# Loads of gate/up weights moved from the end of a block's gate/up into the projections and W2's passes, with new places for key copies, Wo rows, residual tiles and packs

## The chip, the cores and the metric

The kernel runs on one NeuronCore of a Trainium2 chip. TensorE (PE) multiplies, VectorE (DVE), ScalarE (ACT) and GpSimd (POOL) do the elementwise work, and SyncE (SP) issues nearly all DMAs, in the order in which they stand in its program. The metric is the device time of one execution in microseconds; shorter is better.

## What is computed

A layer norm, sliding-window attention and a gated MLP, added to the input:

```python
def _A_ref(x, wqkv, wo):                   # H = 32 heads of Dh = 18, window W = 256
    q, k, v = ...                          # x @ wqkv, split into heads
    scores = einsum("bhqd,bhkd->bhqk", q, k) * Dh**-0.5
    mask = (i - j >= 0) & (i - j < W)
    p = softmax(where(mask, scores, -1e9))
    return (p @ v) @ wo
def _B_ref(x, w1, w3, w2):
    return (silu(x @ w1) * (x @ w3)) @ w2  # 576 -> 4608 -> 576
xn = layernorm(x)                          # x: 1 x 2048 x 576, bf16
return x + _A_ref(xn, A_wqkv, A_wo) + _B_ref(xn, B_w1, B_w3, B_w2)
```

## The kernel before

The 2048 rows are worked in four blocks of 512 (the loop over `c`, line 1296). Each block goes through three stages on TensorE.

**Gate/up.** 36 units (`u`), each 128 of the 4608 hidden columns: nine pairs of matmuls of W3 and W1 with the transposed, normalized input (`unit_pairs`, L855), then ScalarE's tanh (L864) and two VectorE operations that form the gated value (L870, L873). Between the pairs stand the scores, exponentials and masks of attention and, at fixed units, the products of probabilities with V ("PV", L734). In block 0 two PV products stand together in unit 27; the second writes PSUM banks that unit 26 used and VectorE's L873 must free. Four units use one set of W3/W1 columns. A set comes from HBM in four parts (two DMAs of 320 KB and two of 256 KB; the first two sets in six smaller ones) into one of three buffers (`load_part`, L339). Nine sets make a block; block 0's nine come first, and the first two of the next block are asked for at the end of the block ahead.

**Projections.** Q, K and V of the next block (`proj_begin`, L492), nine passes in the order of `PROJ` with a list index `m`. VectorE and ScalarE cast the results to `stage`; from there small DMAs repack queries (`new_q`, from ScalarE's queue) and keys (`new_k`, L633: eight copies of 72, 18 and 9 KB) to the layout that scores need.

**W2's passes.** Four 32-row lanes of TensorE run side by side, in rounds (`w2_lanes`). An output slice of 128 columns takes 36 matmuls of W2 a lane (L1031) and then four or five with Wo's rows and the packed attention output `oT` (L1040). Scores of the next block's first heads are mixed in. W2 comes in pieces of 288 KB into four buffers (`load_w2`, L375); a piece serves nine rounds, and its buffer is asked for again when all four lanes are through with it. Four pieces are loaded ahead in gate/up, so a slice's four pieces are there at the start and the fifth piece, the first of the second slice, is the first that the stage itself loads. The last 64 columns follow in L1081, and a last PV product ends the stage.

What sets the order of DMAs is the order of calls: `add("sp", ...)` appends an instruction to SyncE's program, with waits for the last writer or reader of each buffer. SyncE waits at an instruction until its semaphores are there, and nothing behind it is issued meanwhile. Four places decide it here:

- In gate/up, `owed += 4` at every fourth unit asks for a set; `owe_part` then issues one of its parts after the fourth and the ninth pair of a unit, each waiting for TensorE to come that far.
- `later(u, ...)` puts packs (`o_pack`, L812: four copies of the attention output of two head groups to `oT`), residual additions and stores at fixed units.
- `if c == 0 and u == ...` places block 0's one-time work: the clear of the new-key buffer `kn`, the eight copies of block 0's last 256 keys into it (`first_prev`, L648), Wo's rows (L1465, L1476, L1479) and `wz` (L1481). The normalized tiles of block 1 are transposed by DMA (`xn_send`, L449); a tile buffer `xn0` or `xn1` is written again (L424) only after its transpose has landed.
- In W2's passes a dictionary by round number, `events`, places repacks of the older heads' queries and keys (`span_main`, L580, and `span_last`, L611) and loads of residual tiles (L307).

```python
                if u % 4 == 3 and u < NF - 4 and (c or u != 15) or c and u == 0:
                    owed += 4
```

## Time and profile before

| what | value |
|---|---|
| median of three runs | 557.95 us (556.53 to 558.99) |
| the profiled execution: its time / its span | 558.62 us / 556.9 us |
| TensorE busy | 548.9 us (99%) |
| VectorE / ScalarE / GpSimd busy | 66% / 53% / 22% |
| the chain of work that ended last | PE 94%, DMA 3%, SyncE's queue 1% |
| granted TensorE clock | full throughout |
| gate/up, blocks 0, 1, 2 | 81.7, 75.9, 75.9 us |
| projections, for blocks 1, 2 | 13.8, 13.2 us |
| W2's passes, blocks 0, 1, 2 | 47.6, 45.5, 45.5 us |
| DMA traffic | 88.13 MB, mean 158 GB/s |

All times in the views are microseconds from the start of the span. "SPq" is an issue by SyncE's queue: its start, how long the issue took, and the transfer; the transfer lands later, and "us to landing" counts from the issue's start. A row of a timeline with "x4" holds four neighbours that were merged. "DMA share" is the mean busy share of sixteen DMA engines in a window. Idle time of TensorE is put in brackets with the one that ended it.

### The profile page before, as it was taken

How to read it: one execution, taken by the hardware profiler on the slowest of the kernel's cores; microseconds unless marked ns; L12 is line 12 of the kernel's file. 1: busy time of each engine (PE TensorE's matmuls, PEld its weight loads, DVE VectorE, ACT ScalarE, POOL GpSimd, SP SyncE). 2: the span in 40 equal slices, each digit the busy share in tenths (PEclk: the TensorE clock that was granted, in tenths of full speed). 3: DMA queues.
4: the chain of work that ended last, by engine and by line, in shares of the span. 5: the costliest groups of instructions: out<-in, count | busy, mean ns of one | idle time of the engine just before them, and what ended most of it. 6: DMA issues, size and time to landing. Idle time of an engine off the chain costs nothing.

```text
span 556.9 us, 17711 instructions
## 1 busy us (share of the span) xinstructions
PE 548.9 (99%) x7690; PEld 305.6 (55%) x7690; DVE 365.4 (66%) x745; ACT 294.2 (53%) x481; POOL 120.1 (22%) x281
## 2 busy tenths in 40 slices
PE   8999998989999999999999999999999999999998
PEld 4555554568564444455556444445555644545776
DVE  6566988735747889674664888866465686676211
ACT  6557765348735554536782555443787355554000
POOL 5524645100003332120001242320000222211000
PEclk9999999999999999999999999999999999999999
DMA  9997968967747996994793799697577488662552
GB/s 244 184 207 147 209 146 161 208 148 159 163 68 172 205 206 116 207 181 112 147 168 82 172 209 195 133 208 145 141 148 118 109 191 173 165 150 79 137 151 64
DMA packets 167031, 88.13 MB, mean 158 GB/s; under 512 B 102506, under 2 KB 164714, under 8 KB 166954
## 3 DMA queue, kind: packets, MB, share of 16 engines
q1 hardware_dynamic: 165834, 85.42, 74.6%
q10 hardware_dynamic: 1120, 1.59, 1.0%
q8 instruction: 60, 0.98, 0.8%
q14 instruction: 17, 0.14, 0.1%
HBM read 71.30 MB, written 2.36 MB: 132 GB/s over the span
## 4 chain that ended last, share of the span: by engine, by line
PE 94%; DMA 3%; SPq 1%; DVE 0%; issue 0%
PE ps L855 50%; PE ps L1031 17%; PE ps L492 8%; PE ps L927 6%; PE ps L677 4%; PE ps L1081 2%; PE ps L734 2%; PE ps L1040 2%; PE ps L786 2%; DMA pt<-in_A_wqkv_dram 1%; PE ps L751 1%; DMA w<-in_B_w_dram 1%; PE ps L934 1%; DMA kn<-stage 1%; SPq L633 0%
## 5 line engine op out<-in xcount | busy, mean ns | idle before, releaser
L855 PE MATMUL ps<-xnT,w 64*128 64x512 bf16 x1400 | 177.8, 376 | 1.6 <-issue 1.6
L855 PE MATMUL ps<-xnS,w 64*128 64x512 bf16 x1120 | 148.6, 376 | 0.0
L870 DVE SCALAR_TENSOR_TENSOR gs<-thb,ps 128x512 bf16<-128x512 bf16 x144 | 98.6, 685 | 66.6 <-ACT thb L864 66.1
L864 ACT ACTIVATE thb<-ps 128x512 bf16<-128x512 f32 x144 | 85.6, 595 | 60.7 <-PE ps L855 59.5
L1031 PE MATMUL ps<-hT,w 32*128 32x512 bf16 x1728 | 108.2, 374 | 0.0
L855 PEld LDWEIGHTS ps<-xnT,w 64*128 64x128 bf16 x1400 | 67.5, 94 | 73.2 <-issue 2.1
L873 DVE SCALAR_TENSOR_TENSOR hT<-gs,ps 128x512 bf16<-128x512 bf16 x144 | 98.9, 687 | 5.0
L855 PEld LDWEIGHTS ps<-xnS,w 64*128 64x128 bf16 x1120 | 54.0, 94 | 57.0
L1031 PEld LDWEIGHTS ps<-hT,w 32*128 32x128 bf16 x1728 | 59.8, 92 | 28.5 <-issue 1.4
L758 ACT ACTIVATE pt<-ps 128x512 bf16<-128x512 f32 x120 | 65.2, 594 | 9.6 <-PE ps L751 9.5
L686 ACT ACTIVATE pt<-ps 128x1024 bf16<-128x1024 f32 (+1 forms) x46 | 46.2, 1005 | 41.6 <-PE ps L677 41.6
L751 PE MATMUL ps<-qv,kn 18*128 18x384 bf16 (+2 forms) x288 | 54.5, 268 | 1.6 <-DMA qv<-stage 1.2
L801 POOL TENSOR_TENSOR oq<-uq,rden 128x288 bf16<-128x288 f32 x15 | 10.1, 672 | 202.6 <-DVE rden L800 202.6
L766 DVE TENSOR_TENSOR pt<-pt,kv 128x256 int32<-128x256 int32 x96 | 31.4, 372 | 27.0 <-ACT pt L758 26.4
L713 POOL TENSOR_TENSOR pt<-pt,mk 128x128 int32<-128x128 int32 (+1 forms) x82 | 33.0, 424 | 69.5 <-ACT pt L686 69.4
L492 PE MATMUL ps<-xnT,wp 64*128 64x512 bf16 (+1 forms) x360 | 38.7, 355 | 0.1
L927 PE MATMUL ps<-w,hT 128*128 128x288 bf16 (+1 forms) x292 | 36.9, 284 | 0.0
L686 ACT ACTIVATE hT<-ps 128x1024 bf16<-128x1024 f32 (+1 forms) x20 | 20.0, 1002 | 31.5 <-PE ps L677 31.4
L751 PEld LDWEIGHTS ps<-qv,kn 18*128 18x128 bf16 x288 | 26.3, 93 | 15.2 <-issue 1.7
L927 PEld LDWEIGHTS ps<-w,hT 128*128 128x128 bf16 x292 | 28.2, 98 | 7.3 <-issue 0.2
L677 PE MATMUL ps<-qv,kv 64*128 64x320 bf16 (+4 forms) x336 | 31.7, 258 | 0.0
L808 DVE STREAM_TRANSPOSE od<-oq 128x256 bf16<-128x256 bf16 x64 | 25.2, 424 | 7.5 <-POOL oq L801 6.5
(124 smaller groups left out, 523.7 us busy)
## 6 DMA issues: line engine op xcount, KB each, us to landing
w<-in_B_w_dram SPq DMA_DIRECT2D x66, 320.0 KB, 5.1
w<-in_B_w_dram SPq DMA_DIRECT2D x72, 288.0 KB, 3.8
w<-in_B_w_dram SPq DMA_DIRECT2D x66, 256.0 KB, 5.2
w<-in_B_w_dram SPq DMA_DIRECT2D x12, 192.0 KB, 6.9
xp<-in_A_x_dram SPq DMA_DIRECT2D x4, 576.0 KB, 5.2
xnS<-xnT SPq DMA_DIRECT2D x8, 256.0 KB, 7.3
xp<-in_A_x_dram SPq DMA_DIRECT2D x14, 144.0 KB, 3.4
oT<-od SPq DMA_DIRECT2D x52, 36.0 KB
```

What stands on the lines that cost most here:

```text
L492: op = add("pe", lambda e, out_=out_, st=st, mv=mv, n=n, r0=r0, first=first: e.matmul(out_, st, mv, start=first, stop=(part == 1 and n == ...
L677: add("pe", lambda e, r0=r0, out_=out_, kb=kb, q0=q0, nb=nb: e.matmul(out_, kb4[r0:r0 + 64, g - GN, kb + NV - NB, :] if kb < 0 else kv[r0: ...
L686: add("act", lambda e: e.activation(pt_slot(sl)[:, 0:w, :], PS[:, SC[0]:SC[1] + 1, 0:w].rearrange("p r q -> p q r"), ACT.Exp, scale=scale) ...
L713: add("pool", lambda e, vb=vb, mm=mm: e.tensor_tensor(vb, vb, mm, ALU.mult), r=(key if n == 0 else []) + ["mk"], **{"w" if n == 0 else "j" ...
L751: add("pe", lambda e: e.matmul(PS[:, b, c0:c0 + nb * 128], kn[32 * a:32 * a + Dh, g, W + 128 * jb:W + 128 * jb + 128], qv[32 * a:32 * a + ...
L758: add("act", lambda e: e.activation(head_of(sl, p), PS[:, b, :], ACT.Exp, scale=scale), r=[("ps", b)], **{"j" if p else "w": pt_keys(sl)})
L855: op = add("pe", lambda e, n=n, r0=r0, r=r, k=k, src=src: e.matmul(PS[:, b0 + r, :], wt[r0:r0 + 64, k, fl * 128:(fl + 1) * 128], src, star ...
L864: add("act", lambda e: e.activation(th[i][:], PS[:, bg, :], ACT.Tanh, scale=0.5), r=[("ps", bg)], w=[("th", i)])
L870: add("dve", lambda e: e.scalar_tensor_tensor(out=gs[i][:], in0=th[i][:], scalar=1.0, in1=PS[:, bg, :], op0=ALU.add, op1=ALU.mult), r=[("t ...
L873: add("dve", lambda e: e.scalar_tensor_tensor(out=hT[:, u, :], in0=gs[i][:], scalar=0.5, in1=PS[:, bu, :], op0=ALU.mult, op1=ALU.mult), r= ...
L927: add("pe", lambda e: e.matmul(bank, hT[:, f, tt * 128:(tt + 1) * 128], w2[sl][:, k, n0:n1], start=first, stop=(c + 1 == NC and half == 1 ...
L1031: add("pe", lambda e, b=b, rows=rows, wt=wt, fl=fl, k=k, a=a, first=first: e.matmul(PS[:, b, :], wt[rows, fl, :], hT[rows, k, :], start=fi ...
```

## The change

Six things move; no arithmetic changes, and the order of TensorE and of ScalarE's activations stays word for word.

1. Gate/up of blocks 0 to 2 no longer asks for the next block's first two sets at units 27 and 31 (the bound `NF - 4` becomes `NF - 12`). The first of these sets is asked for in the projections, one part after each pass from `m == 5` on; the second in W2's passes, one part each at rounds 44, 64, 84 and 104.
2. In the projections the fourth pack (`o_pack(3)`) moves from pass 2 to behind the last pass, so behind the new keys and the set's parts. The input swap `xn_swap` moves ahead of leftover `later` work.
3. In W2's passes the nine repacks stand at rounds 24, 30, 36, 42, 48 and then 38, 52, 66, 80 instead of 34, 39, ..., 74.
4. The next block's residual tiles 0 and 1 are loaded in units 1 and 2 of its gate/up instead of at rounds 124 and 130 of W2.
5. In block 0 the clear of `kn` moves from unit 15 to 6, the eight key copies from units 18 to 25 to units 9 to 16.
6. In block 0 the clear of `wz` moves from unit 20 to 12, and Wo's remaining rows and `wz`'s load from unit 22 to 17.

```diff
-                events.setdefault(W2_REPACK + 5 * k, []).append(("repack", k))
+                events.setdefault(W2_REPACK + (6 * k if k < 5 else 14 * k - 32), []).append(("repack", k))
...
-            elif what == "swap":
-                xn_swap(c + 1, ("sp", "sp"))
-            elif c + 2 < NC:
-                t = (c + 2) * TB + what[1]
-                xslot[t] = load_x(t, 4 + what[1])
+            else:
+                load_part()
...
-        W2_EVENTS = {124: (("x", 0),), 130: (("x", 1),)}
-        W2_REPACK, SEND_AFTER = 34, 15
+        W2_REPACK, SEND_AFTER = 24, 15
+        W2_EVENTS = {44 + 20 * k: (("part",),) for k in range(4)}
...
-            loads = {8: (2,), 17: (3,)} if c == 0 else {12: (2,), 15: (3,)}
+            loads = {8: (2,), 17: (3,)} if c == 0 else {1: (0,), 2: (1,), 12: (2,), 15: (3,)}
...
-                if u % 4 == 3 and u < NF - 4 and (c or u != 15) or c and u == 0:
+                if u % 4 == 3 and u < (NF - 4 if c + 1 == NC else NF - 12) and (c or u != 15) or c and u == 0:
                     owed += 4
...
-                if c == 0 and u == 15:
+                if c == 0 and u == 6:
                     add("pool", lambda e: e.memset(kn[:, :, :].bitcast(dt.float32), 0.0),
...
-                if c == 0 and u == 20:
+                if c == 0 and u == 12:
                     add("dve", lambda e: e.memset(wz[:], 0.0), w=["wz"])
-                if c == 0 and 18 <= u < 26:
-                    first_prev((u - 18,))
-                if c == 0 and u == 22:
+                if c == 0 and 9 <= u < 17:
+                    first_prev((u - 9,))
+                if c == 0 and u == 17:
...
                     if m == 0:
+                        xn_swap(c + 1, ("sp", "sp"))
                         for u in sorted(side):
                             for do in side.pop(u):
                                 do()
-                        xn_swap(c + 1, ("sp", "sp"))
...
                         o_turn(7, 1)
-                        o_pack(3, "sp")
...
+                    if m == 5:
+                        owed += 4
                     if 4 <= m < 8:
                         new_q(m - 4, "act")
                     owe_part(last_pe())
+                o_pack(3, "sp")
```

What this makes of SyncE's program is shown at three places. The first is block 0's gate/up, from the last part of the sixth set (`w13_1`) to the transpose of block 1's first tile. Before, the seventh set (`w13_2`) and Wo's rows stand there:

```order
L339 DMA w13_1<-in_B_w1_dram 64x4x512
L339 DMA w13_2<-in_B_w3_dram 64x5x512
L339 DMA w13_2<-in_B_w1_dram 64x5x512
L339 DMA w13_2<-in_B_w3_dram 64x4x512
L339 DMA w13_2<-in_B_w1_dram 64x4x512
L1465 DMA wo<-in_A_wo_dram 126x1x576 x4
L449 DMA_TRANSPOSE xnT<-xn0 128x5x128
```

After, seven key copies (`kn`) stand between them:

```order
L339 DMA w13_1<-in_B_w1_dram 64x4x512
L648 DMA kn<-stage 18x4x256 x3
L339 DMA w13_2<-in_B_w3_dram 64x5x512
L339 DMA w13_2<-in_B_w1_dram 64x5x512
L648 DMA kn<-stage 18x256
L339 DMA w13_2<-in_B_w3_dram 64x4x512
L339 DMA w13_2<-in_B_w1_dram 64x4x512
L1462 DMA wo<-in_A_wo_dram 126x1x576 x4
L648 DMA kn<-stage 18x256 x2
L648 DMA kn<-stage 9x1x256
L449 DMA_TRANSPOSE xnT<-xn0 128x5x128
```

So the first transpose has seven more issues ahead of it. The second place follows at once, up to the transpose of the second tile (`xn1`); `w13_0` is the eighth set here and `od0` the attention output that is packed. Before:

```order
L449 DMA_TRANSPOSE xnT<-xn0 128x5x128
L307 DMA xp<-in_A_x_dram 128x576
L812 DMA oT<-od0 18x1024 x2
L648 DMA kn<-stage 18x4x256
L812 DMA oT<-od0 16x512
L648 DMA kn<-stage 18x4x256
L339 DMA w13_0<-in_B_w3_dram 64x5x512
L339 DMA w13_0<-in_B_w1_dram 64x5x512
L812 DMA oT<-od0 16x512
L449 DMA_TRANSPOSE xnT<-xn1 128x5x128
```

After, the eighth key copy, Wo's remaining rows and `wz`:

```order
L449 DMA_TRANSPOSE xnT<-xn0 128x5x128
L648 DMA kn<-stage 9x1x256
L307 DMA xp<-in_A_x_dram 128x576
L1473 DMA wo<-in_A_wo_dram 2x4x576
L1476 DMA wo<-in_A_wo_dram 64x1x576 x2
L1478 DMA wz<-in_A_wo_dram 64x1x64
L812 DMA oT<-od0 18x1024 x2
L812 DMA oT<-od0 16x512
L339 DMA w13_0<-in_B_w3_dram 64x5x512
L339 DMA w13_0<-in_B_w1_dram 64x5x512
L812 DMA oT<-od0 16x512
L449 DMA_TRANSPOSE xnT<-xn1 128x5x128
```

Up to the second transpose there are now eight key copies where two were, and four more transfers for Wo and `wz`; behind it, up to the ninth set, they are gone. The third place is the end of block 1's projections; `w2_2` and the following are the fifth piece of W2 and on, `od1` the fourth pack. Before:

```order
L456 DMA xnS<-xnT 64x2048 x2
L812 DMA oT<-od1 18x1024 x4
L633 DMA kn<-stage 18x4x512 x3
L633 DMA kn<-stage 18x512 x3
L633 DMA kn<-stage 9x1x512 x2
L375 DMA w2_2<-in_B_w2_dram 128x9x128
L375 DMA w2_3<-in_B_w2_dram 128x9x128
```

After, with the four parts of a gate/up set (`w13_2`) among the key copies and the pack behind both:

```order
L456 DMA xnS<-xnT 64x2048 x2
L633 DMA kn<-stage 18x4x512 x3
L633 DMA kn<-stage 18x512 x3
L339 DMA w13_2<-in_B_w3_dram 64x5x512
L339 DMA w13_2<-in_B_w1_dram 64x5x512
L339 DMA w13_2<-in_B_w3_dram 64x4x512
L633 DMA kn<-stage 9x1x512 x2
L339 DMA w13_2<-in_B_w1_dram 64x4x512
L812 DMA oT<-od1 18x1024 x4
L375 DMA w2_2<-in_B_w2_dram 128x9x128
L375 DMA w2_3<-in_B_w2_dram 128x9x128
```

Twelve issues stood between the input swap and the fifth piece, now it is sixteen, and the four of the pack, which wait for nothing of the projections' results, come last instead of first. Blocks 0 and 2 have the same rows there.

## Prediction

> **What bounds the kernel now.** I read the page first, then busy time by stage, then who TensorE waited for, then the DMA issues of SyncE in order of time at the two places that the change touches, and last the landings of single transfers. The stage table (columns: window, its length, busy time of PE, PEld, DVE, ACT and POOL, granted clock, DMA share, GB/s) has gate/up of blocks 0 and 1, then their Q/K/V projections, then the W2 passes of blocks 0, 1 and 2:
>
> ```profile
> span 556.9 us, 17711 instructions
> 21.40:103.10 81.70, 80.07 (x1017) 41.93 (x1013) 63.81 (x117) 51.69 (x70) 32.55 (x79) 1.00 0.91 174
> 165.50:241.40 75.90, 75.90 (x852) 36.17 (x850) 60.41 (x114) 39.42 (x55) 22.83 (x56) 1.00 0.92 180
> 104.10:117.90 13.80, 13.80 (x169) 8.43 (x162) 8.99 (x21) 4.98 (x13) 1.35 (x2) 1.00 1.03 203
> 242.70:255.90 13.20, 13.20 (x167) 7.74 (x162) 8.67 (x21) 4.98 (x13) 1.34 (x2) 1.00 0.63 141
> 117.90:165.50 47.60, 45.96 (x925) 31.35 (x924) 25.21 (x64) 31.26 (x59) 1.34 (x2) 1.00 0.62 128
> 255.90:301.40 45.50, 45.50 (x924) 26.79 (x923) 25.25 (x64) 31.29 (x59) 1.34 (x2) 1.00 0.67 128
> 391.80:437.30 45.50, 45.50 (x926) 27.02 (x925) 25.24 (x64) 31.29 (x59) 1.34 (x2) 1.00 0.63 121
> ```
>
> TensorE is the bound, and its clock is full throughout. In block 1 its busy time fills gate/up, projections and W2 to the last digit; in block 2 it fills W2 as well. There is nothing to gain there. Only block 0 has slack: 81.70 - 80.07 = 1.63 us in gate/up, 13.80 - 13.20 = 0.6 us in the projections beside block 1, and 47.60 - 45.50 = 2.1 us in W2. So 4.3 us is the most that rearranged loads can give. The waits of PE name the largest of the first and of the last:
>
> ```profile
> PE ps L855 <- issue: 1.6, 1, 1.6
> PE ps L751 <- DMA qv<-stage: 1.2, 1, 1.2
> ```
>
> The first is the ninth gate/up set of block 0. Its last two parts leave SyncE late and land when PE has nothing left to do (timeline of SyncE, landings of that window, timeline of PE):
>
> ```profile
> 89.16 2.11 SPq L339 DMA_DIRECT2D w<-in_B_w_dram  x2
> w<-in_B_w_dram SPq DMA_DIRECT2D x2, 256.0 KB, 4.6
> 95.21 1.04 PE L855 MATMUL ps<-xnT,w 64*128 64x512 bf16 x8 [1.63 <-issue]
> ```
>
> The last part starts some 0.6 us before 91.27 and needs about 4.6, which gives 95.2. The data was asked for late because SyncE, which issues nearly everything in order, was behind.
>
> **What the change does to TensorE.** The order of TensorE, ScalarE and the arithmetic is untouched; only SyncE's queue, one clear of GpSimd and one of VectorE move. Each term is therefore a wait of TensorE that goes or comes.
>
> *Start of W2, blocks 1 and 2.* This is the largest term. In block 1 SyncE, VectorE and TensorE stand like this before the change:
>
> ```profile
> 249.02 3.07 SPq L812 DMA_DIRECT2D oT<-od  x4
> 252.13 6.29 SPq L633 DMA_DIRECT2D kn<-stage  x8
> 258.47 0.47 SPq L375 DMA_DIRECT2D w<-in_B_w_dram  x1
> 250.46 0.69 DVE L504 CAST stage<-ps 128x512 bf16<-128x512 f32 x1 [0.80 <-PE ps L492]
> 264.18 0.37 PE L1040 MATMUL ps<-oT,wo 32*128 32x512 bf16 x1
> 265.04 0.37 PE L1031 MATMUL ps<-hT,w 32*128 32x512 bf16 x1
> 225.33 1.37 SPq L339 DMA_DIRECT2D w<-in_B_w_dram  x2
> ```
>
> W2's fifth piece (L375) is issued at 258.47, after four packs and eight new-key copies, and TensorE wants it at 265.04, when the first output slice's Wo rows (L1040, from 264.18) are nearly done. After the change the key copies are first. They can't start before VectorE's cast of key tile 3 ends at 250.46 + 0.69 = 251.15, so SyncE idles where it now issues packs. From there it issues eight copies (6.29), four gate/up parts (2 x 1.37 = 2.74) and the four packs (3.07), with some 0.1 between groups: 251.15 + 12.1 + 0.1 = about 263.3. So the fifth piece leaves 4.8 us later than now. What is queued behind is every further W2 piece; who waits is TensorE alone, in order. Landings of 288 KB pieces (the median of this stage's fourteen, then two windows within it) and of small packs at the start of block 3:
>
> ```profile
> w<-in_B_w_dram SPq DMA_DIRECT2D x14, 288.0 KB, 4.3
> w<-in_B_w_dram SPq DMA_DIRECT2D x2, 288.0 KB, 3.4
> w<-in_B_w_dram SPq DMA_DIRECT2D x1, 288.0 KB, 5.1
> DMA to landing us min/median/max: 2.5/2.9/3.7
> ```
>
> The fifth piece lands at 263.3 + 4.3 = 267.6, which is 2.6 us after 265.04; with 3.4 it is 1.7, with 5.1 it is 3.4. The last pack starts at about 262.6 and lands near 265.5, 1.3 after TensorE wants it; the Wo rows take 0.86 after it, so this wait lies inside the other and isn't added. I take 2.6 for each block, since the median row is of this very stage: +5.2 us, ends +3.4 and +6.8. The four parts' bytes need not slow the piece: DMA is 0.63 busy in this stage, and they were asked for ahead of it.
>
> *Start of W2, block 0.* The same queue stands there, so the same wait comes, +2.6. The keys leave earlier, since no four packs stand ahead of them, so the 1.2 us wait for queries and the rest of the 2.1 go: net +0.5, ends -0.4 and +1.3.
>
> *Projections of block 0.* 0.6 us goes with the eight gate/up parts that no longer cross them (203 GB/s against 141 in block 1): -0.6, or 0 if VectorE is what holds them.
>
> *End of gate/up, block 0.* The ninth set's late arrival goes, -1.63: no key copy or Wo row is between its parts any more. But those DMAs now stand in front of block 1's second input transpose, with SyncE already busy (timeline of SyncE, then the landing of the second transpose):
>
> ```profile
> 63.57 3.27 SPq L449 DMA_TRANSPOSE xnT<-xn  x1
> ...
> 69.19 0.83 SPq L648 DMA_DIRECT2D kn<-stage  x1
> ...
> 71.58 1.99 SPq L339 DMA_DIRECT2D w<-in_B_w_dram  x2
> ...
> 74.27 1.28 SPq L449 DMA_TRANSPOSE xnT<-xn  x1
> ...
> 80.80 0.43 SPq L1476 DMA_DIRECT2D wo<-in_A_wo_dram  x1
> 81.28 1.28 SPq L1479 DMA_DIRECT2D wo<-in_A_wo_dram  x2
> 82.61 0.53 SPq L1481 DMA_DIRECT2D wz<-in_A_wo_dram  x1
> xnT<-xn SPq DMA_TRANSPOSE x1, 4.3
> ```
>
> The second transpose, now at 74.27, gets six more key copies ahead of it (8 where 2 were: 6 x 0.83 = 5.0) and the four Wo transfers (0.43 + 1.28 + 0.53 = 2.2). Two blocked stretches should shrink, because SyncE comes to them later: the first transpose from 3.27 to 1.28, the two parts from 1.99 to 1.37, together 2.6. That gives 74.27 + 5.0 + 2.2 - 2.6 = 78.9, landing 4.3 later at 83.2. VectorE waits for that landing before it may overwrite the normalized tile, and TensorE waits for VectorE's next gating:
>
> ```profile
> 80.44 0.64 DVE L424 TENSOR_SCALAR xn<-xp,mv,rstd 128x576 bf16<-128x576 bf16 x2
> 81.89 0.69 DVE L873 SCALAR_TENSOR_TENSOR hT<-gs,ps 128x512 bf16<-128x512 bf16 x1
> 82.64 0.32 PE L734 MATMUL ps<-hT,va 64*20 64x320 bf16 x4
> 84.41 0.59 PE L855 MATMUL ps<-xnT,w 64*128 64x512 bf16 x4
> ```
>
> L424 starts at 80.44; L873 ends at 82.58, and the second PV product, which needs the PSUM banks that it frees, starts at 82.64. So there is no slack: VectorE held to 83.2 costs 2.8 us. Without the first transpose's 2.0 us of shrinking it is 4.8. Even with the transpose in time some wait stays: the eighth set stands behind it, its last part leaves at 78.9 + 1.28 + 0.7 = 80.9 and lands 4.6 later at 85.5, against a first use some 0.2 after 84.41, so 0.9. I take +2.8, ends 0.9 and 4.8; behind it the eighth and ninth set are on time.
>
> The rest I put at nothing. GpSimd's clear of the new-key buffer moves to unit 6 and VectorE's small clear to unit 12; GpSimd is busy 32.55 of 81.70 us there, and masks that wait behind the clear have that slack, without which its length would count. The input swap's issue moves ahead of leftovers of which none are left. Residual tiles 0 and 1 of the next block are needed only from unit 8 of its gate/up, and are asked for in units 1 and 2. The second set's four parts in W2 spread 2.7 us of issue over 60 rounds and find the queue waiting for TensorE anyway; cover gone, each costs 0.7.
>
> Sum against the profiled execution (span 556.9, time 558.62): -1.63 + 2.8 - 0.6 + 0.5 + 5.2 = +6.3, so 564.9. That execution is 0.67 above the median of 557.95, so against the median the forecast is 564.2. The low ends give -1.63 + 0.9 - 0.6 - 0.4 + 3.4 = +1.7, so 559.6; the high ends -1.63 + 4.8 + 0 + 1.3 + 6.8 = +11.3, so 569.2.
>
> **The rivals.**
>
> *A: only the queue at W2 binds.* SyncE recovers more of its blocked time near 64 us than I took off and the transpose is in time; W2's pieces land in 3.4. For it: DMA issues there stretch from 0.6 to over 3 us, so my sum is rough. Against it: even so 0.9 stays. That is the row of low ends, 559.6, which can't be told from no change.
>
> *B: faster, because issuing is cheap.* The place is the start of W2. The fifth piece would have to leave by 265.04 - 4.3 = 260.7, so sixteen issues from 251.15 in 9.6 us, 0.60 each. Below that price TensorE never waits there, the transposes are in time as well, and all of block 0's 4.3 us is won: 557.95 - 4.3 = 553.7. Against it stand 6.29 / 8 = 0.79, 3.07 / 4 = 0.77 and 1.37 / 2 = 0.68 for just these DMAs. The Trainium skill, page "DMA: Bandwidth & Descriptors", section "Issuing engines are not separate DMA queues", says that starting DMAs on several engines only saves the sequencer's time of starting them, which is usually small beside the DMA itself; by it the longer queue would cost next to nothing, and 553.7 would be the sum. The trace disagrees here: 0.79 us to issue a copy of at most 72 KB, eight in a row, is not small.
>
> *C: the moved sets also starve W2 later.* W2 of block 1 moves 128 GB/s at a DMA share of 0.67, which is 191 at a full one, so a piece that falls behind one 256 KB part lands 1.4 us later. Were one such landing uncovered in each of three W2 passes, 4.2 us would come on top. For it: such a share is a mean over bursts. Against it: TensorE is by then 2.6 us later, which gives each further piece that much slack. 564.2 + 4.2 = 568.4.
>
> **How the numbers follow.** Forecast 0.62, A 0.2, B 0.06, C 0.12. A measurement of this kernel tells apart about 0.5%, so faster is below 555.2 and slower above 560.7. A is no change, B is faster with one in a hundred of the rest, the forecast and C are slower: 0.07, 0.2, 0.73. The range runs from 559.0, a little under A, to 568.5, just over C; left out are B, the longer half of C and the far high ends.
>
> **What would show it.** In block 1 and 2's W2 the stage grows from 45.5 to about 48, with one gap of PE at the first Wo rows or the fifth piece, released by a DMA; SyncE's fifth W2 piece leaves some 7.4 us after W2's start instead of 2.5. In block 0 no gap is before the ninth set, and VectorE waits at L424 for a transpose. I am wrong if block 1's W2 stays at 45.5 us, or if that piece leaves within 5 us of W2's start.

## The result and the profile after

The changed kernel takes 578.92 us (median of four runs, 576.75 to 583.17) against 558.47 for the kernel before (556.53 to 560.67): 1.037 times as long, 95% interval 1.030 to 1.045. The forecast was 564.2 with a range to 568.5, so the sign was right and the size was not. The profiled execution has a span of 575.0 us where it was 556.9: 18.1 us to account for.

From the page of the kernel after, its span and the chain that ended last, by engine:

```profile
span 575.0 us, 17711 instructions
PE 84%; DMA 10%; DVE 2%; SPq 2%; ACT 1%; issue 1%; POOL 0%; DVEq 0%
```

DMA is now a tenth of the chain, where it was 3%. The chain counts a transfer from its issue on; TensorE itself stood for transfers of the W2 passes some 14 us in all (the waits below). The stages of the kernel after (window, length, busy time of PE, PEld, DVE, ACT and POOL, granted clock, DMA share, GB/s), in the order gate/up, projections and W2 of block 0, then the same of block 1, then W2 of block 2:

```profile
21.00:104.70 83.70, 81.00 (x1085) 49.30 (x1081) 63.35 (x118) 52.29 (x71) 32.38 (x78) 1.00 0.85 169
104.70:118.10 13.40, 13.40 (x178) 7.69 (x162) 9.04 (x21) 4.97 (x13) 1.35 (x2) 1.00 0.32 76
118.10:170.00 51.90, 46.79 (x926) 26.80 (x922) 25.34 (x64) 31.51 (x59) 1.34 (x2) 1.00 0.96 154
170.00:247.10 77.10, 77.10 (x944) 37.20 (x936) 61.01 (x115) 40.01 (x56) 22.82 (x56) 1.00 0.87 164
247.10:260.40 13.30, 13.30 (x174) 7.77 (x162) 8.77 (x21) 4.97 (x13) 1.34 (x2) 1.00 0.30 74
260.40:312.50 52.10, 48.41 (x924) 27.70 (x922) 25.49 (x64) 31.49 (x59) 1.34 (x2) 0.97 0.95 154
403.00:455.30 52.30, 46.83 (x924) 26.82 (x922) 25.27 (x64) 31.52 (x59) 1.34 (x2) 1.00 0.95 153
```

Gate/up of blocks 1 to 3 and the projections for blocks 2 and 3 are as long as before. Nearly everything is in the three W2 passes. From the first matmul of a stage to the first of the next, gate/up of block 0 went from 82.65 to 83.72 us, its projections from 13.84 to 13.41, and W2 from 47.58, 45.46 and 45.46 to 51.85, 52.11 and 52.38. That is +1.07 - 0.43 + 4.27 + 6.65 + 6.92 = +18.5; gate/up of block 0 began 0.38 earlier, which leaves the 18.1. In the passes the DMA share rose from about 0.65 to 0.95, and TensorE, which before never waited in those of blocks 1 and 2, now does. Its waits (engine and line, what it waited for, us in total, times, longest):

```profile
PE ps L1031 <- DMA w<-in_B_w_dram: 9.6, 13, 1.4
PE ps L1040 <- DMA oT<-od: 2.7, 2, 1.5
PE ps L734 <- DVE hT L873: 2.7, 1, 2.7
PE ps L1040 <- issue: 1.6, 1, 1.6
```

The third is the wait of block 0's second attention product, forecast at 2.8. The second and the fourth are the Wo rows at the start of the passes. The first is new: thirteen waits for pieces of W2, not three. Here is the start of block 1's pass, on TensorE and then on SyncE:

```profile
270.05 0.37 PE L1040 MATMUL ps<-oT,wo 32*128 32x512 bf16 x1 [1.20 <-DMA oT<-od]
271.96 0.54 PE L1031 MATMUL ps<-hT,w 32*128 32x512 bf16 x1 [0.87 <-DMA w<-in_B_w_dram]
272.73 2.35 PE L1031 MATMUL ps<-hT,w 32*128 32x512 bf16 x20
```

```profile
261.46 1.46 SPq L339 DMA_DIRECT2D w<-in_B_w_dram  x2
262.96 1.59 SPq L633 DMA_DIRECT2D kn<-stage  x2
264.60 0.67 SPq L339 DMA_DIRECT2D w<-in_B_w_dram  x1
265.31 2.96 SPq L812 DMA_DIRECT2D oT<-od  x4
268.31 1.11 SPq L375 DMA_DIRECT2D w<-in_B_w_dram  x2
273.91 2.16 SPq L580 DMA_DIRECT2D kv<-stage  x1
```

Gate/up parts (L339), the last new keys, the packs and then the fifth piece leave in the forecast order, and the piece leaves 7.9 us after the pass's start at 260.4 (7.4 forecast). TensorE waits 1.20 + 0.87 = 2.07 us for packs and piece. That is the start; what the forecast lacks lies behind it. The landings of W2's pieces in that pass, before and after (issues, KB, median us from issue to landing):

```profile
w<-in_B_w_dram SPq DMA_DIRECT2D x14, 288.0 KB, 4.3
```

```profile
w<-in_B_w_dram SPq DMA_DIRECT2D x14, 288.0 KB, 5.8
```

The same pieces take 1.5 us longer to land. Here is the pass in slices of 5 us, first of before, then of after (columns as in the stage table):

```profile
255.90:260.90 5.00, 5.00 (x99) 2.64 (x101) 1.60 (x5) 3.00 (x7) 0.00 (x0) 1.00 0.38 88
270.90:275.90 5.00, 5.00 (x106) 2.68 (x102) 2.14 (x7) 4.36 (x9) 0.00 (x0) 1.00 0.63 118
280.90:285.90 5.00, 5.00 (x107) 2.66 (x100) 4.21 (x15) 4.23 (x8) 0.67 (x1) 1.00 1.01 160
295.90:301.40 5.50, 5.50 (x125) 4.93 (x121) 2.50 (x4) 0.67 (x2) 0.00 (x0) 1.00 0.12 24
```

```profile
270.40:275.40 5.00, 4.13 (x53) 1.62 (x45) 1.58 (x3) 1.09 (x2) 0.00 (x0) 0.67 1.21 225
280.40:285.40 5.00, 4.88 (x97) 2.31 (x89) 2.32 (x6) 3.95 (x8) 0.00 (x0) 1.00 1.26 157
290.40:295.40 5.00, 4.65 (x92) 2.29 (x88) 3.76 (x14) 3.77 (x7) 0.67 (x1) 1.00 1.44 153
305.40:312.50 7.10, 7.10 (x152) 5.82 (x144) 2.50 (x4) 1.08 (x2) 0.00 (x0) 1.00 0.19 34
```

The mean of 0.67 before hides a middle that already reached 1.01 and an end at 0.12. After, the middle holds 1.0 to 1.4 (the share is the packets' time over sixteen engines, and exceeds 1 where packets overlap), TensorE waits in it, and the end is as empty as it was. In two of these slices the bytes per second are no higher than in the fullest one before (157 and 153 GB/s against 160): there the larger share is packets that took longer, not more that passed.

### The profile page after: what moved, and what is told of

Read it like the earlier page. It is cut to its first block, busy times and chain, and to the rows that moved or that the text cites. A ratio compares the mean times of both kernels' runs of the same rounds, so it can differ in the third digit from the quotient of the medians.

```text
span 575.0 us, 17711 instructions
## 1 busy us (share of the span) xinstructions
PE 553.9 (96%) x7690; PEld 307.7 (54%) x7690; DVE 364.7 (63%) x745; ACT 294.8 (51%) x481; POOL 120.1 (21%) x281
## 4 chain that ended last, share of the span: by engine, by line
PE 84%; DMA 10%; DVE 2%; SPq 2%; ACT 1%; issue 1%; POOL 0%; DVEq 0%
PE ps L855 47%; PE ps L1031 9%; PE ps L492 9%; DMA w<-in_B_w_dram 9%; PE ps L927 6%; PE ps L677 3%; PE ps L734 2%; PE ps L1081 2%; PE ps L786 1%; PE ps L1155 1%; ACT pt L758 1%; PE ps L751 1%; PE ps L934 1%; SPq L339 1%; DMA xnT<-xn 1%
## 5 line engine op out<-in xcount | busy, mean ns | idle before, releaser
L1031 PE MATMUL ps<-hT,w 32*128 32x512 bf16 x1728 | 110.8, 378 | 9.8 <-DMA w<-in_B_w_dram 9.6
L855 PEld LDWEIGHTS ps<-xnT,w 64*128 64x128 bf16 x1400 | 70.8, 94 | 68.2
L855 PEld LDWEIGHTS ps<-xnS,w 64*128 64x128 bf16 x1120 | 56.7, 94 | 54.5
L1031 PEld LDWEIGHTS ps<-hT,w 32*128 32x128 bf16 x1728 | 56.2, 93 | 45.4 <-DMA w<-in_B_w_dram 16.0
L751 PE MATMUL ps<-qv,kn 18*128 18x384 bf16 (+2 forms) x288 | 54.8, 269 | 0.0
L985 DVE TENSOR_TENSOR thb<-ps,thb 128x512 f32<-128x512 f32 x24 | 16.6, 691 | 30.0 <-ACT thb L982 29.4
L751 PEld LDWEIGHTS ps<-qv,kn 18*128 18x128 bf16 x288 | 26.6, 94 | 14.6 <-DVE uq L795 1.4
```

Of the source, the lines that this page charges most:

```text
L751: add("pe", lambda e: e.matmul(PS[:, b, c0:c0 + nb * 128], kn[32 * a:32 * a + Dh, g, W + 128 * jb:W + 128 * jb + 128], qv[32 * a:32 * a + ...
L855: op = add("pe", lambda e, n=n, r0=r0, r=r, k=k, src=src: e.matmul(PS[:, b0 + r, :], wt[r0:r0 + 64, k, fl * 128:(fl + 1) * 128], src, star ...
L1031: add("pe", lambda e, b=b, rows=rows, wt=wt, fl=fl, k=k, a=a, first=first: e.matmul(PS[:, b, :], wt[rows, fl, :], hT[rows, k, :], start=fi ...
```

## Experiments

The first theory, **T**, is that the second moved set, whose four transfers travel inside W2's busy middle, makes pieces land late again and again. Its rivals: **R1**, the late start alone (a ring of four buffers falls behind once and stays behind), and **R2**, the closer small repacks hold SyncE's queue. Each run's median stands beside that of the kernel before, timed on the same chips as that run; those medians lie between 560.09 and 561.43 us (558.47 beside the result). What is said of single waits and passes is read from one profiled execution of each run. "Passes" are the W2 passes of blocks 0, 1 and 2.

**Packs early again** (e1_pack_early).

```diff
                         o_turn(7, 0)
                         o_turn(7, 1)
+                        o_pack(3, "sp")
...
-                o_pack(3, "sp")
                 i_last = (job_ctr - 1) % 3
```

> The changed kernel with the last pack of the heads' outputs issued again behind the third of the projections, as before; everything else stays changed. Theory T (two more sets of gate and up weights travel during each W2 pass, 0.95 of the DMA engines busy against 0.65, so pieces of W2 land late again and again): only the waits for the packed outputs and for the fifth piece at the pass's start get smaller, some 2 us in each pass; the passes go from 51.9, 52.1 and 52.4 us to 49.5 to 51, the whole to 570 to 574 (of 578.9). Rival R1 (the late start alone: the ring of four pieces falls behind once and stays behind, and the later gaps follow from that): the passes are back at 46 to 48 and the whole is within 2 us of 562. Rival R2 (the closer small repacks hold the queue of SyncE): as T or less, under 3 us in all.

577.07 us against 560.18, ratio 1.031 (1.027 to 1.035). Passes 52.13, 51.24, 52.36: hardly shorter. The wait for the packs is gone, but the one for the fifth piece is 3.07, 2.37 and 2.73 us. The piece is issued 5.5 to 6.3 us after the pass's start instead of 7.9 to 8.6, but the gate/up parts now stand right ahead of it and it takes 6.0 to 6.3 us to land instead of 3.5 to 3.6. So moving the pack alone wins nothing at the start: the time that its issues took is traded for a slower landing. T's 570 to 574 is missed as well, and since the start got no shorter, the run doesn't tell T from R1.

**The second set back in gate/up** (e2_second_set_back).

```diff
-        W2_EVENTS = {44 + 20 * k: (("part",),) for k in range(4)}
+        W2_EVENTS = {}
...
-                if u % 4 == 3 and u < (NF - 4 if c + 1 == NC else NF - 12) and (c or u != 15) or c and u == 0:
+                if u % 4 == 3 and u < (NF - 4 if c + 1 == NC else NF - 8) and (c or u != 15) or c and u == 0:
```

> The changed kernel with the second of the two moved sets asked for in gate and up again (at unit 27), so that W2's rounds ask for none; the first moved set stays in the projections. Theory T: half of the added traffic leaves W2; the DMA share of the passes falls from 0.95 to about 0.8 and the gaps behind the first 13 us of each pass go, while the wait for the fifth piece at the start stays: passes of 48 to 49.5 us, the whole 566 to 571. Rival R1: nothing at the start changes, so the later gaps stay too: passes over 51, the whole 576 to 580. Rival R2: as R1.

566.05 against 560.18, ratio 1.013 (1.008 to 1.017). Passes 48.89, 48.52, 47.96. T holds, and R1 falls as the main cause: the start is as late as ever (waits of 1.00 and 0.62 us in block 1), yet 12.9 us of the medians are gone. Landings of the fourteen pieces in that pass are back at a median of 4.3 us. R1 keeps a small share: one later wait for a piece is left in blocks 0 and 1, of 0.43 and 0.75 us.

**Repacks at their old rounds** (e3_repacks_back).

```diff
-                events.setdefault(W2_REPACK + (6 * k if k < 5 else 14 * k - 32), []).append(("repack", k))
+                events.setdefault(W2_REPACK + 5 * k, []).append(("repack", k))
...
-        W2_REPACK, SEND_AFTER = 24, 15
+        W2_REPACK, SEND_AFTER = 34, 15
```

> The changed kernel with the small repacks of queries at their old rounds (34 and every fifth from there) in place of 24 and every sixth, then fourteenth. Rival R2 (these issues hold SyncE's queue when the pieces should be asked for): the passes are shorter by 2 us or more each, the whole 570 or less. Theory T and rival R1: under 1 us a pass either way, the whole 576 to 581.

579.17 against 560.18, ratio 1.036 (1.031 to 1.040). Passes 53.03, 51.56, 52.85: R2's forecast fails. But the run trades one wait for another, so it doesn't clear the repacks by itself. The waits for pieces fall from 9.6 to 6.0 us, and three new ones come, in which TensorE waits for ScalarE's exponentials and these for a repack that now lands late:

```profile
PE ps L1031 <- ACT stage L758: 6.2, 3, 2.4
PE ps L1031 <- DMA w<-in_B_w_dram: 6.0, 8, 1.1
```

```profile
287.36 0.60 ACT L758 ACTIVATE stage<-ps 128x512 bf16<-128x512 f32 x1 [1.84 <-DMA kv<-stage]
```

What clears them as a cause of their own is the next run, which keeps the closer repacks.

**Both sets back in gate/up** (e4_both_sets_back): as the second run, the bound at NF - 4, and

```diff
-                    if m == 5:
-                        owed += 4
```

> The changed kernel with both moved sets asked for in gate and up again (units 27 and 31), nothing in the projections or in W2's rounds; early clears, key copies, Wo rows, residual tiles, the late last pack and the closer repacks stay. Theory T: the DMA share of the passes is back near 0.65, no gap behind the start of a pass; what is left there is the late pack, some 0.5 to 1 us: passes of 46 to 48 us, the whole 558 to 562. The ninth set's late arrival at the end of block 0's gate and up (1.63 us) may be back or not. Rival R1: the late pack still delays the start, passes of 49 or more, the whole 568 or more. Rival R2: passes of 48 or more with gaps between rounds 24 and 100.

560.38 against 560.18, ratio 1.002 (0.998 to 1.007). Passes 48.76, 45.61, 45.91; the first holds a wait of 3.08 us for queries (L751), which was 1.25 before. Their last copy is issued at 116.05 (116.48 before) and TensorE goes on 7.0 us later (5.2), so it is the landing that grew; why, wasn't tried. All else in the change, late packs, early swap, residual tiles, clears, closer repacks, comes to nothing together. The 20 us are the price of the two sets in their new places.

**Only the second set in W2** (e5_first_set_back): the bound at NF - 8, `W2_EVENTS` as changed, the two lines on `m == 5` removed.

> The changed kernel with the first of the two moved sets asked for in gate and up again (unit 27) and none in the projections; the second stays in W2's rounds. So far: both sets back 560.4, only the first moved 566.0, both moved 578.9. If each set has its own price (first 5.7, second 12.9): 573, with passes near 50 us, gaps only behind the first 13 us of a pass. If the price is one of the two together (the queue of DMA engines is full only with both): 563 to 567, passes of 46.5 to 48. No wait at the fifth piece in either case, since no gate and up part stands ahead of it.

568.64 against 560.09, ratio 1.016 (1.012 to 1.021). Passes 49.78, 49.22, 50.24, with no wait at the fifth piece, and all gaps later than 15 us into the pass. The median lies between the two forecasts (573, and 563 to 567); the passes agree with the first, by which each set has its own price. By them it is a sum: 10.7 us over the kernel before with the second set alone, 6.9 with the first alone (the second run), 17.8 with both. By the medians the second costs 8.5 alone and the first 5.9 (566.05 - 560.18), 14.4 of the 20.4 of both; what makes the other 6 isn't settled. The landings in block 1's pass have the same median as with both sets:

```profile
w<-in_B_w_dram SPq DMA_DIRECT2D x14, 288.0 KB, 5.8
```

**Both sets thin** (e6_thin_parts). Each of the eight transfers carries 64 KB instead of 320 or 256; the rest of those weights isn't loaded.

```diff
             k, n, a, b = parts_of[nfill]
             first = a == 0 and n == 0
+            b = a + 1 if thin[0] else b
...
                     if m == 5:
                         owed += 4
+                        thin[0] = 1
...
                 late_pv = w2_lanes(c, live, [*JOBS[(i_last - 1) % 3], *JOBS[i_last]])
+                thin[0] = 0
```

> The changed kernel with every transfer of the two moved sets in its place, but carrying one of the five or four rows of weights (64 KB in place of 320 or 256; so part of the gate and up weights that block 1 to 3 multiply by are those of an earlier set). Issues and their order stay, bytes go. Theory T as bytes: the DMA share of the W2 passes falls below 0.75, landings go back to 4 us and SyncE no longer stands; passes of 46 to 47.5, the whole 560 to 563. Theory T as issues (SyncE's time of issuing, and the place of the parts ahead of the fifth piece, as the prediction worked it out: 2.7 us of issue ahead of it in each block): the wait of 2 to 2.6 us at the start stays, passes of 48 to 50, the whole 566 to 571.

569.69 against 560.09, ratio 1.016 (1.011 to 1.022). Passes 49.47, 49.09, 50.42 at DMA shares of 0.66 to 0.75. The start's waits stay (2.93 us, 1.74 and 1.75), so the first set's price there is its place and issue time, as forecast. The whole comes out where the forecast by issues had it (566 to 571), not at the 560 to 563 by bytes: of the 17.8 us that the passes grew, 7.4 go with the bytes. Later gaps remain too, one of 1.3 to 1.6 us near 18 us into the passes of blocks 1 and 2 and another of 0.96 in block 2. The run mixes two things, a late start and four issues in W2's rounds; the thirteenth run has the second without the first.

**The second set on ScalarE's queue** (e7_second_set_on_act).

```diff
             else:
-                load_part()
+                load_part(eng="act")
```

> The changed kernel with the four transfers of W2's rounds issued by ScalarE's queue in place of SyncE's; the bytes, their rounds and the first set stay. If bytes are the price: passes stay at 51 to 53 us, the whole 576 to 581. If SyncE's queue is (a part that waits to be issued holds the next piece of W2 behind it): passes fall to what they are without the second set, 48 to 49 us, the whole 566 to 569. Cost of its own: ScalarE issues for about 0.7 us each beside its exponentials, which may hold a score step, under 1 us a pass.

580.58 against 560.09, ratio 1.037 (1.032 to 1.041). Passes 53.38, 51.89, 52.71. Taking the four issues off SyncE saves nothing, and TensorE has no wait for ScalarE in their place: their hold on SyncE's queue isn't what costs.

**Both sets back, block 0's edits undone** (e8_sets_and_block0_back): as the fourth run, with the clears, key copies and Wo rows at units 15, 20, 18 to 25 and 22.

> The kernel with both sets back in gate and up, and in addition the edits of block 0 undone (clears, key copies and Wo rows at their old units); what is left of the change is the late last pack, the residual tiles, the input swap and the closer repacks. Forecast by the terms of block 0: the wait of the second attention product for VectorE (2.25 us with both sets back) goes, the ninth set's late arrival (1.63 before the change) returns; gate and up of block 0 is 82.3 to 82.9 us (83.07 without this edit), the whole within 1.5 us of 560.4. Rival: the late pack and the swap cost or save over 2 us by themselves: the whole is outside 558 to 562.

562.28 against 560.09, ratio 1.004 (1.001 to 1.007). Gate/up of block 0 is 84.91 us, worse than the 82.3 to 82.9 forecast, and the whole lies just outside its forecast too: the wait of the second attention product falls from 2.25 to 0.71, but the ninth set is 3.14 us late where it had been 1.63. The two places trade with each other, as the prediction had it, at prices that move by over a microsecond with what else is queued.

**Key copies on ScalarE's queue, on the kernel before** (e9_copies_on_act).

```diff
-                    add("sp", lambda e, dst=dst, src=src: e.dma_start(dst, src), r=st_keys(*tset), dma="knp",
+                    add("act", lambda e, dst=dst, src=src: e.dma_start(dst, src), r=st_keys(*tset), dma="knp",
```

> The kernel before, with one edit: the eight copies of earlier keys in block 0 are issued by ScalarE's queue instead of SyncE's, at their old units 18 to 25. It asks whether block 0's slack (4.3 us by the prediction's count) can be had without touching W2. If SyncE's backlog is what delays the ninth set there: 8 x 0.85 = 6.8 us of issues leave SyncE before the ninth set, its late arrival (1.63 us) and the 0.4 us of the projections behind it go, nothing else changes: 2 us faster than before, gate and up of block 0 about 81 us. If ScalarE's issues delay its activations (about 0.75 us each): one or two waits of TensorE for ScalarE of under 1 us each, and no gain.

554.98 against 560.37, ratio 0.993 (0.990 to 0.997): the only version here that moves all its bytes and beats both kernels. Its first three stages and the one wait of its TensorE behind the kernel's first 2 us:

```profile
21.20:102.20 81.00, 80.99 (x1086) 42.22 (x1082) 64.08 (x118) 52.36 (x71) 32.51 (x78) 1.00 1.03 181
102.20:115.60 13.40, 13.40 (x169) 7.68 (x170) 9.04 (x21) 4.97 (x13) 1.35 (x2) 1.00 0.89 193
115.60:161.70 46.10, 45.75 (x926) 31.37 (x926) 25.16 (x64) 31.25 (x59) 1.34 (x2) 1.00 0.66 132
```

```profile
PE ps L751 <- DMA kn<-stage: 0.4, 1, 0.4
```

Block 0's slack is nearly all taken: its busy time fills gate/up, with no wait of ScalarE in its place. SyncE's backlog in gate/up was the limit. The profiled executions are 3.7 us apart (556.9 and 553.2), within the 4.3 that the prediction counted as slack; the medians are 5.4 apart. Among the runs at full mean clock (ten before, nine here) the medians are 558.3 and 554.8, so 3.5 apart; the rest comes from runs with windows of halved clock (1.7 us each, below), which are rarer here.

**Wo rows there too** (e10_copies_rows_on_act): the four small transfers of unit 22 also on ScalarE's queue.

> As the run with the key copies on ScalarE's queue, and also the four small Wo transfers of unit 22 (2.2 us of issue). If SyncE's backlog is what counts: 0 to 1 us less than that run, at most 3 us faster than before. If ScalarE is the dearer place: slower than that run.

558.52 against 560.37, ratio 0.999 (0.996 to 1.001), so worse than the run before it. TensorE waits 1.6 us once for ScalarE's exponentials, and the ninth set is 2.3 us late again.

**The second set at the end of the pass** (e11_second_set_late).

```diff
-        W2_EVENTS = {44 + 20 * k: (("part",),) for k in range(4)}
+        W2_EVENTS = {148 + 4 * k: (("part",),) for k in range(4)}
```

> The changed kernel with the second set's four transfers at rounds 148, 152, 156 and 160 of the W2 pass in place of 44, 64, 84 and 104; nothing else. The trace of before has the DMA engines busy 0.63 to 1.01 from 5 to 40 us of W2 and 0.12 in its last 5.5 us. If the bytes cost because they fall in that busy stretch: the passes are as without the second set, 48 to 49 us, the whole 564 to 568. If four more transfers in a pass cost wherever they are: 576 to 580. If they come too late for the first units of the next gate and up: a wait of TensorE there, W2 short and gate and up longer by the same.

569.33 against 560.37, ratio 1.018 (1.013 to 1.023). Most of the second set's price goes, though not all: passes 49.74, 49.02, 49.92, against 48.89, 48.52 and 47.96 without it. One window of halved clock (1.7 us, below) is in the first of these. Block 2 still has a gap of 1.36 us at 18 us into the pass, ahead of any of these transfers. The piece waited for is issued 12.6 us into the pass, as in the second run (12.5), where it landed in 5.5 us and nobody waited; here it took 6.7, and 7.1 in the sixth run, which has the same gap. With a late start it arrives with no slack; why its landing varies isn't settled.

**Both sets at the end** (e12_both_sets_late): none at `m == 5`, `W2_EVENTS` at rounds 128, 132, 136, 140, 148, 152, 156 and 160.

> The changed kernel with both moved sets at the end of the W2 pass: the first at rounds 128 to 140 and none in the projections, the second at 148 to 160. If only the place of the transfers costs (the first set ahead of the fifth piece, the second in the busy stretch): passes of 45.5 to 46.5 us, and the whole as with both sets in gate and up, 559 to 562. If the first set, needed at once in the next gate and up, comes too late: a wait of TensorE at the start of gate and up of 1 us or more in blocks 1 to 3. Block 0's wait for VectorE (2.2 to 2.9 us) stays in either case.

565.08 against 560.37, ratio 1.012 (1.006 to 1.018). Neither forecast had this: the start is clean and so is the next gate/up, and the wait has moved to the last piece, for the last 64 columns. It stands behind the first set's parts, takes 5.2 to 6.4 us to land (3.7 to 4.8 before) and is late in all three passes (49.70, 47.55, 47.40).

```profile
PE ps L1081 <- DMA w<-in_B_w_dram: 5.6, 3, 2.4
```

**The second set alone, thin** (e13_second_set_thin): as the fifth run, with the transfers of W2's rounds cut as in the sixth.

> Only the second set in W2's rounds (the first asked for in gate and up, as in the run at 568.6), and its four transfers carry one of five or four rows of weights each, 64 KB (so part of the gate and up weights of blocks 1 to 3 are those of an earlier set). If its bytes are the price: the passes fall from 49.2 to 50.2 us to 45.6 to 46.5, the whole 560 to 563. If its issues are, between the pieces of W2: passes stay over 48.5, the whole over 567. Between the two: the share of each is read off.

558.63 against 561.43, ratio 0.996 (0.993 to 0.999). This settles it for the second set alone. The four issues stand at the same places between W2's pieces, at 64 KB each, and the passes are those of the kernel before:

```profile
119.60:165.10 45.50, 45.50 (x926) 26.90 (x922) 25.30 (x64) 31.29 (x59) 1.34 (x2) 1.00 0.77 130
255.60:301.00 45.40, 45.40 (x924) 27.28 (x922) 25.23 (x64) 31.29 (x59) 1.34 (x2) 1.00 0.75 130
391.50:437.80 46.30, 45.69 (x925) 26.95 (x924) 25.22 (x64) 31.29 (x59) 1.34 (x2) 1.00 0.80 127
```

The pieces land in a median of 4.2 us again. Issuing costs nothing there; bytes cost 3.8 to 4.3 us a pass (49.78, 49.22, 50.24 less 45.49, 45.46, 46.28). Behind a late start, as in the sixth run, that isn't shown.

**Both sets behind the last piece** (e14_both_sets_last): as the twelfth run, at rounds 146, 148 and so on to 160.

> As the run with both sets late in W2, but all eight transfers stand behind the last piece of W2 in SyncE's queue (rounds 146 to 160). If only the place costs: no wait in the passes (45.5 to 46 us); the first set is asked for some 6 us before the next gate and up and its last part, fourth of eight, lands about 5 us after its issue, so gate and up starts with at most 1 us of waiting; the whole 559 to 562, the rest over the kernel before being block 0's wait for VectorE. Rival: the first set is late, gate and up of blocks 1 to 3 begins with a wait of 2 us or more each, the whole 566 or more.

561.52 against 561.43, ratio 1.002 (0.999 to 1.005). No loss against the kernel before, and no gain: the wait moves once more, to the first unit of the next gate/up, of 1.19 and 1.49 us in blocks 1 and 2; block 2's pass has one of 0.95 for a piece. The row of block 2's gate/up:

```profile
305.17 1.04 PE L855 MATMUL ps<-xnT,w 64*128 64x512 bf16 x8 [1.49 <-issue]
```

## Why the prediction was wrong, step by step

**Start of W2, blocks 1 and 2 (+2.6 each): right.** The fifth piece left as forecast, the waits there are 2.07 and 1.95 us, and the passes with only the first set moved are 2.9 and 2.1 us longer than with neither (48.52 - 45.61, 47.96 - 45.91). The packs alone don't make the wait: with packs late but no parts there is none. Nor is it their issue time alone: without the packs between, the piece lands 2.4 us or more slower right behind the parts (the first run). So the prediction's "need not slow the piece" holds only with the packs' issues, 2.96 us, in between; that the parts' bytes are what slows it otherwise is likely, but wasn't tried.

**Start of W2, block 0 (+0.5): at its high end.** With the first set alone, 48.89 - 47.58 = +1.3.

**Projections of block 0 (-0.6): right,** -0.43.

**End of gate/up, block 0 (-1.63 + 2.8): right in the mechanism, lucky in the size.** The ninth set's gap is gone. The second transpose of the kernel after, VectorE held by it, and TensorE behind that:

```profile
79.74 1.28 SPq L449 DMA_TRANSPOSE xnT<-xn  x1
83.27 0.64 DVE L424 TENSOR_SCALAR xn<-xp,mv,rstd 128x576 bf16<-128x576 bf16 x2 [2.97 <-DMA xnT<-xn]
85.28 0.32 PE L734 MATMUL ps<-hT,va 64*20 64x320 bf16 x4 [2.70 <-DVE hT L873]
```

The forecast landing was 83.2 and the wait 2.8; the stage grew by 1.07 where 1.2 was forecast. Two errors cancel in this: the transpose left at 79.74, not 78.9, and landed in 3.4 us, not 4.3. And seven runs that leave this stage's instructions as they are (the first, third, sixth, seventh, eleventh, twelfth and fourteenth) have waits there of 0.97 to 3.84 us and a stage of 81.8 to 87.1, windows of halved clock included, so one execution couldn't have borne out 1.2 to a tenth.

**"The second set's four parts in W2 spread 2.7 us of issue over 60 rounds and find the queue waiting for TensorE anyway": this step failed.** It put the second set at nothing and left out the bytes. On issues it is true where the pass starts in time, as the thin set alone shows. Behind the first set's late start that stays open: with both sets thin the three passes take 3.6 us more than with the first set alone (148.98 against 145.37), but the gap at 18 us that is part of it also stands in the eleventh run, where none of the four is issued by then. On top of the first set, the second lengthens the passes by 51.85 - 48.89, 52.11 - 48.52 and 52.38 - 47.96: 2.96 + 3.59 + 4.42 = 11.0 us of the 17.8 that W2 grew; the first set's 6.9 stand against the 5.7 forecast. "Cover gone, each costs 0.7" priced the smaller resource.

The arithmetic that was missing is that of the ring. W2 has four buffers, and within an output slice TensorE uses up one piece in about 2.17 us (block 1 before: pieces begun at 287.94, 290.11 and 292.27). A buffer is refilled when its piece is done and wanted again three pieces later, 6.5 us. A landing of 4.3 leaves 2.2 for SyncE to come to it; one of 5.8 leaves 0.7. One repack holds SyncE for 2.16 us (at 273.91 above), which by this sum the first just bears and the second doesn't. The trace agrees where the queue was longest: the two longest waits of blocks 0 and 2, 1.22 and 1.40 us, are for a piece issued right behind two repacks and a part of the second set, which took 5.6 and 5.7 us to land.

**Rival C named this and priced it at little more than a third.** It took one uncovered landing of 1.4 us a pass, 4.2 in all, with a chance of 0.12. The 1.4 was right (the median landing grew by 1.5), the count wrong: not one piece a pass was late but thirteen in three passes, the fifth pieces among them. Two things misled. The DMA share of 0.67 was a mean over a middle at 0.6 to 1.0 and an empty end. And the argument against it, that TensorE is by then 2.6 us later "which gives each further piece that much slack", is wrong for a ring: a piece is asked for when TensorE has used up its buffer, so the requests are as late as TensorE is.

**Residual tiles, clears, swap, repacks (0): right** when taken together, as the fourth run shows at 560.38 against 560.18.

**Not in the sum at all: the clock.** In block 1's pass, right behind the two waits, TensorE ran at half its clock for 3.4 us, which is 1.7 us lost. Two of the other three runs after have a mean clock of 0.994 where the profiled one has 0.997; if the same holds there, they had two such windows.

## What to carry to other kernels

Price a transfer that is moved by the stretch that it lands in, in slices of a few microseconds, and by what it does to the landings of the ring that feeds TensorE: buffers less one, times the use of a piece, less the landing, is all the delay that the queue may have. A moved load is free only where that difference stays positive; here even the pass's empty end had a reader waiting behind it. Where one engine's queue has a backlog, moving small issues to another's can win what reordering them can't (5.4 us at the medians), until that engine is itself waited for.

## What the runs showed of the hardware

**Half the clock after a stretch that was only partly idle.** The granted clock of these profiles is 0.50 in sixteen windows of 3.41 us ahead of the kernels' last 5 us, always on one grid of 3.41 us that runs through the whole execution. Rows of PE's busy time in such windows, of the kernel after (a window, then the next), of the run with both sets thin, of the one with the second set late, and of the one with packs early:

```profile
268.70:272.10 3.40, 1.33 (x24) 0.50 (x24) 0.63 (x2) 0.58 (x1) 0.00 (x0) 1.00 0.91 185
272.10:275.50 3.40, 3.40 (x37) 1.44 (x33) 1.68 (x3) 1.09 (x2) 0.00 (x0) 0.50 1.16 204
...
80.90:84.30 3.40, 1.68 (x80) 0.89 (x74) 1.03 (x3) 0.02 (x1) 0.61 (x2) 1.00 1.11 216
84.30:87.70 3.40, 2.42 (x88) 1.54 (x90) 3.37 (x7) 1.02 (x2) 0.70 (x2) 1.00 0.66 147
```

```profile
126.80:130.20 3.40, 1.49 (x31) 0.66 (x23) 1.05 (x3) 1.93 (x4) 0.00 (x0) 1.00 0.20 47
130.20:133.60 3.40, 2.38 (x44) 1.04 (x48) 0.00 (x0) 0.69 (x2) 0.00 (x0) 1.00 1.19 236
```

```profile
126.54:129.95 3.41, 1.44 (x31) 0.61 (x23) 1.05 (x3) 1.88 (x4) 0.00 (x0) 1.00 0.43 87
129.95:133.36 3.41, 3.07 (x32) 1.09 (x36) 0.00 (x0) 0.27 (x1) 0.00 (x0) 0.50 1.16 234
```

```profile
82.00:85.50 3.50, 0.70 (x64) 0.46 (x40) 1.88 (x5) 0.00 (x0) 0.00 (x0) 0.99 1.00 183
85.50:88.90 3.40, 3.31 (x82) 1.79 (x84) 2.71 (x6) 0.92 (x1) 0.67 (x1) 0.50 0.66 168
```

Busy for 1.33 of 3.41 us, idle 61%, for 1.44, idle 58%, or for 0.70: the next window is at half clock. Busy 1.68 or 1.49, idle 51 or 56%: it is not. Taken over every grid window from block 0's gate/up to those last 5 us, in all profiles here but the tenth run's, whose clock never changes and so shows no grid, each of the fifteen with TensorE idle 58% or more was followed by a half-clock window, and of those idle 56% or less none was, but for one that was itself already at half clock. 58% of 3.41 is 2.0 us, and a boundary can split a wait of up to twice that. So by estimate a wait of about 2 to 4 us costs 1.7 us more (half of 3.41) or nothing, by where it falls on the grid: the 2.70 us wait at 82.6 in the kernel after straddled a boundary and cost only itself, one of 2.89 us at the same place in the run with packs early cost 1.7 more. The Trainium skill, page "TensorE: Matmul & The Clock Gate", Part 1, has the window's length (3413 ns, free-running) and half clock after at least one idle window; the grid agrees, but the window here need not be idle, 58% of it was enough.

**Issuing is not cheap, and two queues help or don't by what is short.** The Trainium skill, page "DMA: Bandwidth & Descriptors", section "Issuing engines are not separate DMA queues", says that spreading issues over engines saves only the sequencer's time, usually little. For W2's bytes the runs agree: on ScalarE's queue the second set costs as much (580.58 against 578.92). For small copies, 0.8 us of SyncE each, they don't: there the sequencer's time was what was short, and the move gained 0.7%.
